# Attention by pairs of heads, with whole float32 score products on two halves of the array's rows

## The chip, the cores and the metric

The kernel runs on one core of a Trainium2 chip. The core has a matrix engine (TensorE; in the profile PE for the products and PEld for loading their stationary operand), a vector engine (DVE), a scalar engine (ACT), GpSimd (POOL), and SyncE (SP), whose queue issues all the DMAs here. Each engine works through its own instructions in program order, and semaphores tie the engines together. The metric is the time of the whole program on the device in microseconds (us).

## The reference

Capped softmax attention over 4 batches of 12 heads (448 positions, head size 64), then two feed-forward networks over the 1792 tokens:

```python
scores = (q @ k.T) / sqrt(64)                    # per batch and head: 448 x 448
scores = cap * tanh(scores / cap)                # cap = 30
attn = exp(scores - max(scores, axis=-1))
attn = attn / (sum(attn, axis=-1) + 1e-09)
x = concat_heads(attn @ v)                       # 1792 x 768
h = maximum(x @ w_in, 0);  x = (h * h) @ w_out   # 768 -> 2048 -> 768
g = x @ w_gate                                   # 768 -> 1536
out = (g * sigmoid(g) * (x @ w_val)) @ w_out2    # 1536 -> 768
```

The weights arrive as 64-bit floats; inputs q, k, v and the output are float32.

## The kernel before

**Feed-forward.** A batch (448 tokens) is the moving operand, 128 x 128 blocks of weights are the stationary one. To keep float32 accuracy on the `float32r` path, weights and activations are split into a high and a low part (`w_hi`, `w_lo`; `x_hi`, `x_lo`; `g_hi`, `g_lo`), and `unit_mm` (L595) sums three products, high·high, high·low and low·high. There are 4896 such matmuls of 448 columns, in three passes over the weights: pass 0 takes batches 0 and 1 together and decodes the 64-bit weights on DVE (L563 to L565: three integer instructions a unit) while storing the decoded copy to DRAM; pass 1 takes batch 2 and pass 2 batch 3 with the stored copy.

**Attention.** Scores are kept transposed: keys on the partitions (4 chunks of 112), queries along the free axis. Per head (`h`), in two steps `u` of two key chunks each: `scores` (L266, or L263 for the very first pair of heads), `tanh` on ACT from PSUM (L168), the maximum over the chunks on DVE (`tree`, L176 and L177), the maximum over the 112 partitions on POOL (`reduce`, L186: 448 elements wide), subtraction on DVE (`sub`, L190), `exp` on ACT (L194). Then the row sums and the product with v (`av`, L286: two heads side by side in two 64-column halves of the array), the reciprocal (`recip`), `norm`, and the split into `x`.

Scores also go through `float32r`: `hi` (ACT, L136) and `lo` (DVE, L140) split q and k, and `stack` (L157) moves the parts by DMA, so that the 128 rows of the array hold the high part of 64 dimensions of one head over its low part. Two matmuls with the high and the low part of q on both halves give one 112 x 448 block, four give a step `u`. The PSUM tile `s` (two banks) has one buffer.

Batches 0 and 1 (12 pairs of heads) come before the feed-forward, with nothing else to do ("early" below). There q and k are transposed on PE (`early_tr`), the result of POOL is copied by ACT into PSUM (`early_m`, L271: tile `mp`), so `sub` reads one operand from SBUF and one from PSUM, and the row sums are products of `ones` with each chunk (`row_sum`, L302). Batches 2 and 3 ("late") are spread between the feed-forward matmuls of passes 0 and 1; there q and k are transposed on DVE, `sub` reads the tile `mr` in SBUF, and DVE adds the four chunks up (`total`, L314 and L316) before one product with `ones` a head (`total_sum`, L324).

**What sets the order.** `early_attention` is a list schedule with a table of priorities (`PRIO`): an operation goes to its engine when its inputs and buffers are free by the table's durations. The late attention and the feed-forward are laid out by times: `plan_head` puts each step at an offset (`STEP`) from the time of its scores, and all events are emitted sorted by time.

Of the kernel before, what the change touches and what calls it, by code (L numbers as in the profile page):

```python
# [18 lines left out]
DRAM = bass.MemoryType.DRAM  # L19


@with_exitstack
def kernel(
# [17 lines left out]

    nc = tc.nc
# [11 lines left out]


    PRIO = dict(
        st=-1276.1, stj=95.8, ld=-54.4, lv=478.5, tr=-26.9, sc=-34.5, tree=-70.1, par=1194.4,
        m=-55.8, sub=50.5, exp=-11.6, av=-67.0, rc=253.2, norm=140.7, xh=261.1, w=-9.5,
        ws=462.4, wi=27.3,
    )  # L60
    STEP = dict(
        ld=-46.02, ldv=-8.42, pr=-14.3, st1=2.7, u1=2.2, mx=2.99, par=7.2, exp=2.5, av=5.6, av1=1.1,
        tot=1.86, sm=2.3, rs=6.8, rs1=6.18,
    )
    LEAD, TAIL = [17.2, 15.7], [60.0, 35.0]
    WEIGHT = [{'1b': 0.6, '2b': 0.6, 'end': 0.0}, {'end': 1.0}]
    NPRE, NWARM, GB = 3, 50, 10
    LAG = 0.2
# [33 lines left out]
    c_abs = capt[:CP, 1:2]  # L102
    c_inv = capt[:CP, 2:3]


    MM = S / 2.4e3 + 0.003
    EARLY = 2
    raw_t, pair_t, head_t = {}, {}, {}
    v_busy = [False, False]
    x_done = {}  # L110

    def att_load(b, p):
        kr = ap.tile([P, TB, 32], F32, tag="kr", name="kr")
        qr = ap.tile([P, TB, 32], F32, tag="qr", name="qr")
        for t, src in ((kr, k), (qr, q)):
            for j in range(2):
                for e in range(2):
                    g = 2 * j + e
                    nc.sync.dma_start(
                        t[32 * g : 32 * g + 32],  # L120
                        src[b, 2 * p + j, :, 32 * e : 32 * e + 32].rearrange("(t r) d -> r t d", r=32),
                    )
        raw_t[b, p] = dict(k=kr, q=qr)

    def att_tr(b, p, x):
        d = raw_t[b, p]
        d[x + "T"] = ap.tile([P, S], F32, tag="tT", name=x + "T")
        V.transpose(out=d[x + "T"], in_=d[x].rearrange("p t d -> p (t d)"))

    def src_t(b, p, x):  # L130
        d = raw_t[b, p]
        return d["ps" + x][:, :S] if b < EARLY else d[x + "T"]
# [11 lines left out]
    def stack(b, p, x, j):  # L144
        hl = f32(raw_t[b, p]["hl" + x])
        r = slice(64 * j, 64 * j + 64)
        if x == "k":
            t = ap.tile([P, S], F32R, tag="ks", bufs=4, name="ks")
            src = (hl[r, 0], hl[r, 1])
        elif b < EARLY:  # L150
            t = fp.tile([P, 2, S], F32R, tag=f"acc{j}", bufs=3, name="qs")
            src = (hl[r], hl[r])
        else:
            t = ap.tile([P, 2, S], F32R, tag="qs", bufs=2, name="qs")
            src = (hl[r], hl[r])
        for i in range(2):
            nc.sync.dma_start(f32(t[64 * i : 64 * i + 64]), src[i])  # L157
        head_t.setdefault((b, 2 * p + j), {})[x] = t

    def att_begin(b, h):  # L160
        t = ap.tile([CP, NC, S], F32, tag="al" if h % 2 else "ah", name="tt")
        head_t[b, h]["t"] = [t[:, 2 * i : 2 * i + 2] for i in range(2)]

    def tanh(b, h, u):
        d = head_t[b, h]
        if b < EARLY:
            d.setdefault("t", []).append(fp.tile([CP, 2, S], F32, tag="g", bufs=GB, name="te"))
# [28 lines left out]
    def x_hi(b, c, src):
        A.copy(xbuf[b % 2][c][:, 0], src())

    def x_lo(b, c, src, on=None):
        x = xbuf[b % 2][c]  # L200
        (on or V).tensor_tensor(x[:, 1], src(), f32(x[:, 0]), ALU.subtract)  # L201
        x_done[b, c] = x_done.get((b, c), 0) + 1


    def early_load(b, p):
        raw_t[b, p] = {}
        if (b, p) == (0, 0):
            n = ap.tile([CP, 2, 2, NC, D], F32, tag="ah", name="kqn")
            for j in range(2):
                for x, src in (("k", k), ("q", q)):  # L210
                    raw_t[0, 0][x] = n[:, "kq".index(x)]
                    nc.sync.dma_start(raw_t[0, 0][x][:, j], src[0, j].rearrange("(p c) d -> p c d", c=NC))
            return
        n = ap.tile([CP, 2, NC, 2, D], F32, tag="al" if p % 2 else "ah", name="kqn")
        for x, src in (("k", k), ("q", q)):
            t = raw_t[b, p][x] = n[:, "kq".index(x)]
            nc.sync.dma_start(t, src[b, 2 * p : 2 * p + 2].rearrange("j (p c) d -> p c j d", c=NC))

    def load_v(b, p):
        order = "j (p c) d -> p j c d" if b < EARLY else "j (c p) d -> p j c d"  # L220
        nc.sync.dma_start(vt[p % 2], v[b, 2 * p : 2 * p + 2].rearrange(order, c=NC))
        assert not v_busy[p % 2]
        v_busy[p % 2] = True
        pair_t[b, p] = dict(v=vt[p % 2])

    def transposes(pt, x, src):
        for c in range(NC):
            col = slice(c * CP, (c + 1) * CP) if x == "k" else slice(c, S, NC)
# [639 lines left out]
```

## Time and profile before

| | |
|---|---|
| three runs, median (lowest to highest) | 1274.63 us (1272.74 to 1274.97) |
| the profiled execution | 1278.07 us, its span 1276.3 us |
| PE busy | 1238.7 us, 97% of the span |
| DVE busy | 925.9 us, 73% |
| ACT busy | 586.9 us, 46% |
| POOL busy | 83.7 us, 7% |
| mean granted clock of TensorE | 0.988 |
| chain that ended last | PE 83%, DVE 9%, DMA 3%, ACT 3% |
| feed-forward matmuls in that chain (L595) | 70% |

A matmul's length in the profile includes the time until its result leaves the array, so neighbours overlap; what a matmul costs its successors is the distance between starts. A whole float32 matmul shows as two records, each of one part of the product; the order of instructions counts it once. Shares over the whole span mix the early stage, in which PE has gaps, with the later ones, in which it has nearly none, so the stages are to be read apart.

### The profile page before, as it was taken

How to read it: one execution, taken by the hardware profiler on the slowest of the kernel's cores; microseconds unless marked ns; L12 is line 12 of the kernel's file. 1: busy time of each engine (PE TensorE's matmuls, PEld its weight loads, DVE VectorE, ACT ScalarE, POOL GpSimd, SP SyncE). 2: the span in 40 equal slices, each digit the busy share in tenths (PEclk: the TensorE clock that was granted, in tenths of full speed). 3: DMA queues.
4: the chain of work that ended last, by engine and by line, in shares of the span. 5: the costliest groups of instructions: out<-in, count | busy, mean ns of one | idle time of the engine just before them, and what ended most of it. 6: DMA issues, size and time to landing. Idle time of an engine off the chain costs nothing.

```text
span 1276.3 us, 17347 instructions
## 1 busy us (share of the span) xinstructions
PE 1238.7 (97%) x6348; PEld 1048.2 (82%) x6348; DVE 925.9 (73%) x1449; ACT 586.9 (46%) x895; POOL 83.7 (7%) x59
## 2 busy tenths in 40 slices
PE   7889899999999899999999999999999999999997
PEld 5544469889798699898898988897898899999997
DVE  5899987767877887779888756887866833465344
ACT  4788765435334324333142376554454354433431
POOL 1223210000001001001000010010010000000000
PEclk8999899999999899999999999999999999999999
DMA  7877627556573575874765875457354443343333
GB/s 177 212 176 181 152 69 202 160 166 182 149 221 108 146 208 137 231 183 113 236 168 131 228 154 145 121 141 165 103 135 121 113 125 112 107 127 105 108 91 85
DMA packets 235365, 191.28 MB, mean 150 GB/s; under 512 B 144336, under 2 KB 197904, under 8 KB 235280
## 3 DMA queue, kind: packets, MB, share of 16 engines
q1 hardware_dynamic: 235280, 190.17, 55.6%
q8 instruction: 50, 0.82, 0.3%
q14 instruction: 35, 0.29, 0.1%
HBM read 124.85 MB, written 33.62 MB: 124 GB/s over the span
## 4 chain that ended last, share of the span: by engine, by line
PE 83%; DVE 9%; DMA 3%; ACT 3%; issue 2%; SPq 1%; DVEq 0%; POOL 0%; POOLq 0%; ACTq 0%
PE ff L595 70%; PE sc L266 5%; PE av L286 5%; DVE te L190 1%; PE rs L302 1%; DMA qs<-hl 1%; PE rs L324 1%; DVE mx L176 1%; DVE wp L582 1%; DVE acc L641 1%; DVE x L201 1%; ACT te L168 1%; DVE wx L564 1%; PE tr L229 1%; ACT te L194 1%
## 5 line engine op out<-in xcount | busy, mean ns | idle before, releaser
L595 PE MATMUL ff<-x,wp 128*128 128x448 f32 x2880 | 595.3, 365 | 1.4 <-DVE x L201 1.4
L595 PEld LDWEIGHTS ff<-x,wp 128*128 128x128 f32 x2880 | 538.9, 188 | 52.3 <-issue 6.4
L595 PE MATMUL ff<-g,wp 128*128 128x448 f32 x2016 | 420.5, 367 | 1.5 <-DVE g L633 1.5
L595 PEld LDWEIGHTS ff<-g,wp 128*128 128x128 f32 x2016 | 378.2, 188 | 42.1 <-issue 7.8
L582 DVE TENSOR_TENSOR wp<-wx,wp 128x768 fp32r<-128x768 f32 (+1 forms) x246 | 207.7, 844 | 139.7 <-ACT wp L577 134.7
L577 ACT CAST wp<-wx 128x768 fp32r<-128x768 f32 (+1 forms) x246 | 177.5, 722 | 253.3 <-PE ff L595 161.4
L186 POOL PARTITION_ALL_REDUCE mr<-mx x48 | 81.2, 1692 | 902.4 <-DVE mx L177 869.3
L266 PE MATMUL sc<-qs,ks 128*112 128x448 f32 x368 | 95.2, 381 | 15.6 <-ACT te L168 11.6
L641 DVE TENSOR_TENSOR acc<-ff,acc 128x448 f32<-128x448 f32 x120 | 74.0, 618 | 41.0 <-PE ff L595 40.6
L266 PEld LDWEIGHTS sc<-qs,ks 128*112 128x112 f32 x368 | 61.9, 178 | 42.5 <-ACT te L168 21.6
L633 DVE TENSOR_TENSOR g<-gg,g 128x448 fp32r<-128x448 f32 x112 | 69.3, 618 | 13.7 <-ACT g L629 13.5
L629 ACT CAST g<-gg 128x448 fp32r<-128x448 f32 x112 | 63.1, 564 | 34.4 <-DVE gg L625 33.8
L610 ACT ACTIVATE r<-ff 128x448 f32<-128x448 f32 x64 | 34.8, 544 | 84.4 <-PE ff L595 84.2
L616 ACT ACTIVATE th<-ff 128x448 f32<-128x448 f32 x48 | 26.1, 544 | 96.7 <-PE ff L595 96.6
L564 DVE SCALAR_TENSOR_TENSOR wx<-wr,wx 128x512 int32<-128x512 int32 (+1 forms) x82 | 68.1, 830 | 2.8
L565 DVE SCALAR_TENSOR_TENSOR wx<-wr,wx 128x512 int32<-128x512 int32 (+1 forms) x82 | 67.4, 822 | 2.8
L620 DVE SCALAR_TENSOR_TENSOR sg<-th,ff 128x448 f32<-128x448 f32 x48 | 29.7, 619 | 52.8 <-ACT th L616 52.8
L168 ACT ACTIVATE te<-sc,capt 112x896 f32<-112x896 f32 x48 | 48.2, 1004 | 28.7 <-PE sc L266 21.3
L625 DVE SCALAR_TENSOR_TENSOR gg<-ff,sg 128x448 f32<-128x448 f32 x48 | 29.9, 622 | 36.7 <-PE ff L595 36.4
L194 ACT ACTIVATE tt<-tt,capt 112x896 f32<-112x896 f32 x48 | 48.9, 1042 | 7.4 <-DVE tt L190 7.4
L639 ACT COPY acc<-ff 128x448 f32<-128x448 f32 x48 | 25.6, 534 | 56.1 <-PE ff L595 56.1
L194 ACT ACTIVATE te<-te,capt 112x896 f32<-112x896 f32 x48 | 48.9, 1038 | 5.2 <-DVE te L190 4.9
(63 smaller groups left out, 818.3 us busy)
## 6 DMA issues: line engine op xcount, KB each, us to landing
wx<-w SPq DMA_DIRECT2D x80, 384.0 KB, 3.1
wx<-w SPq DMA_DIRECT2D x84, 256.0 KB, 2.6
qs<-hl SPq DMA_DIRECT2D x92, 224.0 KB, 3.8
w<-wx SPq DMA_DIRECT2D x40, 384.0 KB, 2.7
wr<-in_moe_w_in_dram SPq DMA_DIRECT2D x16, 768.0 KB, 5.5
wr<-in_moe_w_out_dram SPq DMA_DIRECT2D x24, 512.0 KB, 4.1
w<-wx SPq DMA_DIRECT2D x42, 256.0 KB, 2.2
ks<-hl SPq DMA_DIRECT2D x92, 112.0 KB, 2.9
```

Of the source, the lines that this page charges most:

```text
L186: G.partition_all_reduce(d["m"], d["mx"][:, 0], CP, bass_isa.ReduceOp.max)
L194: A.activation(t, t, AF.Exp, scale=c_abs)
L266: PE.matmul(ps[:CP, i, :S], d["k"][:, cols], d["q"][:, s], start=(s == 0), stop=(s == 1))
L286: PE.matmul(d["ps"][64 * j : 64 * j + 64, :S], d["v"][:, j, c], head_t[b, 2 * p + j]["t"][u][:, c % 2], start=(c == 0), stop=(c == NC - 1),)
L564: V.scalar_tensor_tensor(x, hi, -0x40000000, x, ALU.bitwise_and, ALU.bitwise_or)
L565: V.scalar_tensor_tensor(x, lo, 29, x, ALU.logical_shift_right, ALU.bitwise_or)
L577: A.copy(hl[:, 0], raws[ps, i])
L582: (on or V).tensor_tensor(hl[:, 1], raws[ps, i], f32(hl[:, 0]), ALU.subtract)
L595: PE.matmul(ffn_ps[i, b][:, :S], hl[:, h, c], x[:, t], start=(c == 0 and s == 0), stop=(c == cnt(u) - 1 and s == 2),)
L629: A.copy(g_t[b, f][:, 0], tmp_t[i, b])
L633: (on or V).tensor_tensor(g[:, 1], tmp_t.pop((i, b)), f32(g[:, 0]), ALU.subtract)
L641: V.tensor_tensor(acc, pt, acc, ALU.add)
```

## The change

- One class `Plan` replaces both ways of ordering: every operation of the program has an engine, a duration, a rank (its wished time), inputs and buffers, and `order` hands out the earliest operation that can start.
- Attention works on a pair of heads at a time. q and k of a pair lie in one tile `kT` (128 partitions: head 0 on the lower 64, head 1 on the upper), copied from PSUM by ACT in the early stage, transposed by DVE in the late one. `hi`, `lo`, `stack` and their DMAs are gone.
- `scores` (L228) does one key chunk of both heads: two whole float32 matmuls with 64 contraction rows each, in the lower and the upper row half of the array, each into a PSUM bank of its own. In the early stage, chunks take turns between the PSUM tiles `s` and `a`.
- Maximum, reduction, subtraction, exponential and (late) sum work on 112 x 896 tiles, both heads side by side: three `top` (L245), one `reduce` (L250) of 896 elements, four `sub` (L256) a pair; late, three `total` (L282) and one group of four sum matmuls (L290) just ahead of the eight `av` matmuls (L303).
- `sub` reads the reduced maximum from SBUF in both stages; the copy to PSUM is gone.
- The decode of a unit's weights is three operations instead of one, pass 0 starts with three units of batch 0 and then three of batch 1, and passes 1 and 2 load weights into five buffers instead of four.

```diff
+class Plan:
+    def order(self, free):
...
+        while len(seq) < len(ops):
+            best = None
+            for eng, some in ready.items():
+                first = None
+                for i in some:
+                    _, _, _, rank, _, _, _, alloc, _ = ops[i]
+                    t = max(since[i], free[eng])
...
+                    if t < 1e9 and (first is None or (t, rank) < first[:2]):
+                        first = t, rank, i
+                if first and (best is None or (first[0], first[2]) < (best[0], best[2])):
+                    best = first
...
-    def hi(b, p, x):
-        t = raw_t[b, p]["hl" + x] = ap.tile([P, 2, S], F32R, tag="hl", bufs=2, name="hl")
-        A.copy(t[:, 0], src_t(b, p, x))
-
-    def lo(b, p, x):
-        t = raw_t[b, p]["hl" + x]
-        V.tensor_tensor(t[:, 1], src_t(b, p, x), f32(t[:, 0]), ALU.subtract)
...
+    def tr_copy(b, p, i):
+        A.copy(kt(b, p)[:, i], pair[b, p].pop(("tr", i))[:, :S])
...
+    def scores(b, p, c, tag):
+        d = pair[b, p]
+        pool = ps_s if tag == "s" else ps_a
+        ps = d["s", c] = pool.tile([P, 2, 512], F32, tag=tag, name="sc")
+        for j in range(2):
+            r = slice(64 * j, 64 * j + 64)
+            PE.matmul(
+                ps[:CP, j, :S], d["kT"][r, 0, c * CP : (c + 1) * CP], d["kT"][r, 1], start=True, stop=True
+            )
...
-    def tree(b, h):
...
-        V.tensor_tensor(mx, d["t"][0], d["t"][1], ALU.max)
-        V.tensor_tensor(mx[:, 0], mx[:, 0], mx[:, 1], ALU.max)
...
+    def top(b, p, c):
+        d = pair[b, p]
+        if c == 1:
+            d["mx"] = ap.tile([CP, 2, S], F32, tag="mx", bufs=2, name="mx")
+        V.tensor_tensor(d["mx"], d["t", 0] if c == 1 else d["mx"], d["t", c], ALU.max)
...
+    def sub(b, p, c):
+        d = pair[b, p]
+        V.tensor_tensor(d["t", c], d["t", c], d["m"], ALU.subtract)
...
-    def early_m(b, h):
-        d = head_t[b, h]
-        ps = ps_a.tile([P, 512], F32, tag=f"a{h % 2}", name="mp")
-        A.copy(ps[:CP, :S], d["m"])
-        d["m"] = ps[:CP, :S]
...
+    def total(b, p, c):
+        d = pair[b, p]
+        if c == 1:
+            d["sm"] = ap.tile([CP, 2, S], F32, tag="mx", bufs=2, name="sm")
+        V.tensor_tensor(d["sm"], d["t", 0] if c == 1 else d["sm"], d["t", c], ALU.add)
...
+    def total_sum(b, p):
+        d = pair[b, p]
+        d["a"] = ps_a.tile([P, 2, 512], F32, tag="a", name="av")
+        d["rs"] = d["a"][:, 1]
...
+            add(K("sc", c), "PE", 0.78, at + 8 + c, scores, (b, p, c, tag), deps, [(tag, 1, [K("th", c)])], pe)
...
+        add(K("par"), "POOL", 3.2, at + 13, reduce, (b, p), [K("top", 3)], [("m", 2, [K("sub", 3)])])
```

Where the work stands is shown at two places. The first is PE in pass 0, at the first late pair of heads (`ff` are feed-forward products, `sc` scores, `rs` row sums, `sm` the sums that DVE made, `av` the product with v). Before:

```order
L266 MATMUL sc<-qs,ks 112x448 x4
L595 MATMUL ff<-g,wp 128x448 x12
L266 MATMUL sc<-qs,ks 112x448 x4
L595 MATMUL ff<-g,wp 128x448 x36
L266 MATMUL sc<-qs,ks 112x448 x4
L595 MATMUL ff<-g,wp 128x448 x12
L266 MATMUL sc<-qs,ks 112x448 x4
L595 MATMUL ff<-g,wp 128x448 x48
L324 MATMUL rs<-sm,ones 32x224 x2
```

and now, from the third scores group of the pair on:

```order
L228 MATMUL sc<-kT 112x448 x2
L453 MATMUL ff<-x_0_85,wp 128x448 x3
L453 MATMUL ff<-x_1_86,wp 128x448 x3
L453 MATMUL ff<-x_2_87,wp 128x448 x3
L228 MATMUL sc<-kT 112x448 x2
L453 MATMUL ff<-x_3_88,wp 128x448 x3
L453 MATMUL ff<-x_4_89,wp 128x448 x3
L453 MATMUL ff<-x_5_90,wp 128x448 x3
L453 MATMUL ff<-g,wp 128x448 x63
L290 MATMUL av<-sm,ones 32x224 x4
L303 MATMUL av<-tt,v 64x448 x8
```

The four scores groups of a pair stood 12 to 36 feed-forward matmuls apart and now stand 9 apart; the sums, two groups before (the second between the two halves of `av`), are one group ahead of `av`, 72 feed-forward matmuls behind the last scores.

The second place is DVE in the early stage, about pairs 2 to 4 (`mx` maximum, `te` and `tt` tanh tiles, `mp` and `mr` the reduced maximum in PSUM and in SBUF, `hl` the low part of q or k, `st`, `rc`, `rb` the reciprocal, `xs` and `x_n` the output of attention). Before:

```order
L176 TENSOR_TENSOR mx<-te 112x896
L177 TENSOR_TENSOR mx<-mx 112x448
L140 TENSOR_TENSOR hl<-tr,hl 128x448 x2
L201 TENSOR_TENSOR x_2_83<-xs,x_2_83 128x448
L190 TENSOR_TENSOR te<-te,mp 112x896 x2
```

and now:

```order
L245 TENSOR_TENSOR mx<-mx,tt 112x896
L245 TENSOR_TENSOR mx<-te 112x896
L315 STREAM_TRANSPOSE st<-rs 128x224
L319 TENSOR_SCALAR rc<-st 128x14
L322 TENSOR_SCALAR rc<-st 32x7 x4
L326 RECIPROCAL rc<-rc 128x14
L329 STREAM_TRANSPOSE rb<-rc 128x448
L245 TENSOR_TENSOR mx<-mx,te 112x896
L256 TENSOR_TENSOR te<-te,mr 112x896 x2
```

The last maximum of a pair (the first row of each piece ends or holds it) releases POOL's reduction; what DVE did meanwhile mostly read a PSUM operand (`tr`, `mp`), and is now another pair's maximum, with both operands in SBUF.

## Rows read from the trace of the kernel before

**Rows 1.** Stages: window, length, then busy us (instructions) by engine, PEclk, DMA share, GB/s.
```profile
20.00:180.00 160.00, 142.66 (x969) 82.10 (x967) 147.36 (x246) 122.01 (x160) 38.75 (x24) 0.96 0.67 159
416.00:428.00 12.00, 8.53 (x30) 3.65 (x29) 10.50 (x17) 4.33 (x7) 0.00 (x0) 0.72 0.44 136
428.00:722.00 294.00, 294.00 (x1457) 262.20 (x1456) 239.83 (x376) 95.04 (x145) 10.08 (x6) 1.00 0.65 178
```

**Rows 2.** Waits of PE after 200 us: who for whom, total us, times, longest.
```profile
PE rs L324 <- DVE sm L316: 4.1, 2, 3.5
```

**Rows 3.** Groups of DVE: line, operation, tiles, shapes, count | busy us, mean ns.
```profile
L140 DVE TENSOR_TENSOR hl<-tr,hl 128x448 fp32r<-128x448 f32 x22 | 13.0, 615 | 2.8 <-ACT hl L136 2.8
L176 DVE TENSOR_TENSOR mx<-te 112x896 f32<-112x896 f32 x24 | 26.1, 1086 | 5.4 <-ACT te L168 5.2
L177 DVE TENSOR_TENSOR mx<-mx 112x448 f32<-112x448 f32 x48 | 30.0, 625 | 1.7
L190 DVE TENSOR_TENSOR te<-te,mp 112x896 f32<-112x896 f32 x48 | 49.6, 1078 | 0.4 <-ACT mp L271 0.4
L190 DVE TENSOR_TENSOR tt<-tt,mr 112x896 f32<-112x896 f32 x48 | 50.7, 1085 | 0.0
```

**Rows 4.** PE in order of time at 308 us: start us, length us, instruction.
```profile
307.32 0.77 PE L595 MATMUL ff<-x,wp 128*128 128x448 f32 x3
307.93 0.97 PE L266 MATMUL sc<-qs,ks 128*112 128x448 f32 x4
308.74 0.57 PE L595 MATMUL ff<-x,wp 128*128 128x448 f32 x2
```

**Rows 5.** The same view at 335 us.
```profile
334.87 1.72 PE L286 MATMUL av<-tt,v 112*64 112x448 f32 x8
336.53 0.57 PE L324 MATMUL rs<-sm,ones 112*32 112x224 f32 x4
337.03 1.72 PE L286 MATMUL av<-tt,v 112*64 112x448 f32 x8
338.69 0.47 PE L595 MATMUL ff<-g,wp 128*128 128x448 f32 x1
```

**Rows 6.** Within the first row of that group, from three narrow windows.
```profile
334.87 0.60 PE L286 MATMUL av<-tt,v 112*64 112x448 f32 x2
...
335.30 0.92 PE L286 MATMUL av<-tt,v 112*64 112x448 f32 x4
...
335.68 0.92 PE L286 MATMUL av<-tt,v 112*64 112x448 f32 x4
```

**Rows 7.** PE near the start: whole float32 scores of the first pair.
```profile
15.98 1.76 PE L263 MATMUL sc<-qs,ks 96*112 96x448 f32 x4
17.58 1.05 PE L482 MATMUL warm<-zero 128*128 128x128 f32 x8
```

**Rows 8.** DVE and POOL in order of time, in four windows.
```profile
61.23 1.08 DVE L190 TENSOR_TENSOR te<-te,mp 112x896 f32<-112x896 f32 x1
61.48 1.60 POOL L186 PARTITION_ALL_REDUCE mr<-mx  x1 [5.18 <-DVE mx L177]
...
307.22 3.04 POOL L186 PARTITION_ALL_REDUCE mr<-mx  x1 [83.25 <-DVE mx L177]
...
319.03 1.83 POOL L186 PARTITION_ALL_REDUCE mr<-mx  x1 [8.77 <-DVE mx L177]
319.50 1.17 DVE L316 TENSOR_TENSOR sm<-sm,tt 112x448 f32<-112x448 f32 x1
...
320.70 0.62 DVE L316 TENSOR_TENSOR sm<-sm,tt 112x448 f32<-112x448 f32 x1
```

**Rows 9.** PE around the longest of its late waits.
```profile
421.55 0.96 PE L324 MATMUL rs<-sm,ones 112*32 112x224 f32 x4 [3.47 <-DVE sm L316]
422.45 3.25 PE L286 MATMUL av<-tt,v 112*64 112x448 f32 x8
425.63 2.54 PE L595 MATMUL ff<-g,wp 128*128 128x448 f32 x7
```

More of the change, by code (lines that the diff above doesn't have):

```diff
@@ L1 @@
-import heapq
 import math
@@ L53 @@
     FG = 4
[L56 to L68, printed above, removed]
+    EARLY = 2
+    GB, TBUF, NPRE, NWARM = 10, 4, 3, 30
+    FIRST = [17.0, 16.0]
+    LAST = [60.0, 35.0]
     const = ctx.enter_context(tc.tile_pool(name="const", bufs=1))
@@ L100, in set_cap @@
         V.tensor_scalar(capt[:, 2:3], capt[:, 2:3], QS, None, ALU.mult)
[L102 to L118, printed above, removed]
+    pair = {}
@@ L196, in x_hi @@
[L196 to L228, printed above, removed]
-            PE.matmul(pt[:, col], src(c), ident[:CP, :CP], start=True, stop=True, is_transpose=True)
@@ L328, in total_sum @@
+    def total_sum(b, p):
+        d = pair[b, p]
+        d["a"] = ps_a.tile([P, 2, 512], F32, tag="a", name="av")
+        d["rs"] = d["a"][:, 1]
+        for g in range(4):
+            j, i = divmod(g, 2)
+            PE.matmul(
+                d["rs"][32 * g : 32 * g + 32, : S // 2],
+                ones,
+                d["sm"][:, j, i * (S // 2) : (i + 1) * (S // 2)],
                 start=True,
@@ L479, in warm @@
[L479 to L494 removed]
+        d = pair.pop((b, p))
@@ L759, with warm @@
-    early, end = early_attention()
-    t_ffn = max(end[k] for k in end if k[0] in ("av", "mm"))
-    rel = {x: [-1e9] * 3 for x in ("wp", "wr", "wx")}
-    rel["wrx"], rel["wrp"] = [], []
-    t = 0.0
-    for t0, o in early:
-        at(t0 - t_ffn, o["fn"], *o["a"])
-        if o["eng"] == "PE" and t0 > t_ffn:
-            on_pe(t0 - t_ffn, lambda now, d=o["dur"]: d)
+    warm_t = {}
+    def warm(i):
+        if i == 0:
+            warm_t[0] = ps_f.tile([P, 512], F32, tag="f", name="warm")
+        PE.matmul(warm_t[0][:, :P], zero, zero, start=True, stop=True)
@@ L768 @@
+    PAIR = 7.6
+    steps = []
+    t = T0 = 11.0 * EARLY * KD + 8.0
+    gates = {}
     for ps, (bs, seq) in enumerate(passes):
[L769 to L770 removed]
         order = [(i, b) for i in range(NB) for b in bs]
         if ps == 0:
[L773 to L784 removed]
+            order = [(i, b) for b in bs for i in range(NPRE)] + order[NPRE * len(bs) :]
+        lens = [MM3 * cnt(seq[i]) for i, _ in order]
+        heads, spent, at = 0, 0.0, t
+        room = sum(lens) - FIRST[min(ps, 1)] - LAST[min(ps, 1)]
@@ new lines @@
+    for ps, i, b, _ in steps:
+        users.setdefault((ps, i), []).append(b)
+    add(("ident",), "POOL", 8.0, -99, lambda: None)
+    add(("cap",), "DVE", 0.8, -99, set_cap, (), [])
+    for n in range(EARLY * KD):
+        plan_pair(n, 10.6 * n)
+    for i in range(NWARM):
+        add(("warm", i), "PE", 0.43 if i < 8 else 0.22, 1e4 + i, warm, (i,), [("warm", i - 1)] if i else [],
+            [("f", 4, [("warm", NWARM - 1)])] if i == 0 else [])
+    for n, (step, at) in sorted(gates.items()):
+        plan_pair(n, at - 10.0, [("mm", *step[:3], 0)])
@@ L841 @@
+    with tc.manual_schedule():
+        V.memset(zero, 0.0)
+        make_identity(nc, ident)
+        nc.sync.dma_start(capt[:, 0:1], cap[None, :].to_broadcast([P, 1]))
+        G.memset(ones, 1.0)
+        seq = plan.order(dict(PE=0.4, ACT=2.0, DVE=2.6, POOL=0.5, SP=0.0))
+        for _, n in seq:
+            plan.ops[n][4](*plan.ops[n][5])
 _INS = ["q", "k", "v", "cap", "moe_w_in", "moe_w_out", "moe2_w_gate", "moe2_w_val", "moe2_w_out"]
```

854 lines of the change are left out of this document (379 added, 475 removed).

## The prediction

> **What bounds the kernel now.** I read the busy time by stage first, since shares over the span mix unlike stages. From 428 to 722 us PE is busy in all of its 294 us; there only work taken off PE counts. From 20 to 180 us DVE is the fuller engine, 147.36 of 160 us, and PE stands at 142.66 with its overlapping tails counted in [rows 1]. So the early attention goes at DVE's pace, and what DVE does for a pair of heads sets the time, while late only PE's own work and its waits do. Second I read who waits for whom after 200 us: PE waits 4.1 us in all for the sums that DVE makes, 3.5 us of them at once [rows 2]. [...] The `av` group then takes 3.25 us instead of 1.72, the row sum 0.96 instead of 0.57 [rows 5, 9]. Third come the groups of DVE by shape, and last the order in time at PE, for what a visit of attention costs between feed-forward matmuls.
>
> **Early: what DVE loses and gains.** Per pair before: two low parts at 13.0/22 = 0.59 us, two wide maxima at 26.1/24 = 1.09, two narrow ones at 30.0/48 = 0.63, four subtractions at 49.6/48 = 1.03, in sum 8.73 us [rows 3]. Now: three wide maxima, 3.26, and four subtractions from an operand in SBUF, 50.7/48 = 1.06 each [rows 3], 4.22: 7.48 us. The rest (reciprocal, norm, split of x) is the same. 12 pairs x 1.25 us = 15.0 us less.
>
> Against that stands POOL. At 61.48 us a reduction runs 1.60 us beside a subtraction that reads PSUM, and the subtraction takes its usual 1.08 us. At 319.03 us another runs beside a sum of two SBUF operands: that takes 1.17 us, and the same instruction behind it 0.62 [rows 8]. So a reduction of 448 elements holds such an instruction for 0.55 us. Before, the early stage hardly met this: its subtractions read the PSUM copy, its low parts the PSUM transposes. Now the subtractions read SBUF, and the reduction is 896 wide. In the order of DVE, in 9 of 12 early pairs the instruction behind the last maximum reads two SBUF operands. The trace has no 896-wide reduction. The bounds are 0 (as at 61.48) and two holds of twice the length, 2.2 us a pair; I take one hold of twice the length in 9 of 12 pairs, 0.83 us, nearest to the row at 319.50: 12 x 0.83 = 9.9 us. Early net: -15.0 + 9.9 = -5.1 us.
>
> [...]
>
> The transposes' copies go from ACT and DVE to ACT alone, the PSUM copies of the maximum leave ACT; ACT is busy 122.01 of 160 us [rows 1], so I count nothing. If DVE's pace fell to ACT's, the 15.0 could not be had in full. DVE also idles 12.6 us from 20 to 180 us [rows 1]. Without the DMAs of `stack` behind q and k, and with two PSUM tiles for the scores, some of that goes, but three engines are now close to each other in load, and the order of each is fixed beforehand: -2 us, between 0 and -6.
>
> **Late: PE's visits.** Matmuls of 448 columns follow each other at 0.203 us (307.32 to 307.93, three). A scores visit of four costs 308.74 - 307.93 = 0.81 us [rows 4]. In the whole float32 `av`, two products start together in the two column halves, and the next two 0.38 us later (335.30 to 335.68) [rows 6]; a float32 product is two such parts. No row shows two row halves at once; the nearest is this pair of column halves. From it, the two products of a scores visit take 2 x 0.38 = 0.76 us. Entering and leaving such a layout costs something too: from the end of the slot before 334.87 to 338.69 there are 8 steps of `av` and two half steps of sums, 9 x 0.38 = 3.42 of 3.82 us [rows 5], so 0.4 us for the changes, and I take 0.14 each. A visit is then 0.76 + 0.28 = 1.04 us: 48 late visits x 0.23 = +11.0 us. The upper bound is the halves one behind the other: at the start two whole float32 score products take 17.58 - 15.98 = 1.60 us [rows 7]; with the changes 1.88.
>
> The sums and `av` of a pair were one visit of about 3.9 us [rows 5] and one lone sum visit of about 0.6 (one step of 0.38 and two changes). Now one visit: one step, 8 steps of `av`, three changes, 9 x 0.38 + 0.42 = 3.8. That is -0.7 x 12 = -8.4 us. Late visits: +2.6 us.
>
> **Late: the wait for the sums.** Behind the last scores PE has 72 feed-forward matmuls, 14.6 us, and the visit's 1.04: 15.7 us. The chain that has to fit: scores 1.2 with their tail, tanh taken as long as a subtraction, 1.1, last maximum 1.09, reduction 2 x 1.60 [rows 8], four subtractions 4.2, three sums of 896 at the price of a maximum, 3.3: 14.1 us, and DVE's weight work comes in between, as do POOL's holds. If a sum is late, all of PE's feed-forward stands behind it in order. I take 0.5 us a pair, 6 us (bounds 0 and 18). What goes is the one long wait and its slow stretch: 4.1 [rows 2] plus 1.5 for `av`, 0.4 for the sums and 1.0 for seven feed-forward matmuls that take 2.54 us [rows 9], 7.0 us. Net -1.0.
>
> **Sum.** -5.1 - 2 + 2.6 - 1.0 = -5.5 us. The profiled execution has 1278.07 us (span 1276.3), which is 3.4 above the median of the runs; it becomes 1272.6, and the median 1274.63 becomes 1269.
>
> **Rivals.**
> *The row halves take turns.* For it: no row shows them together. Against: the column halves do run together [rows 6], and the two products write different PSUM banks. Price: 48 x (1.88 - 0.81) = +51, sums -8.4, and early 0.84 us x 4 more of PE a pair, 40 us against 17 us of gaps [rows 1], so DVE's gain turns to some +10: near 1325 us. It decides from a visit of about 1.1 us on.
>
> *POOL and DVE hold each other (the slower side).* Place: the early chain maximum, reduction, subtraction, and the same chain late. For it: at 307.22 us a reduction took 3.04 us instead of 1.60 [rows 8], so POOL is held as well. Price: two holds of 1.1 us a pair early, 26.4 - 15.0 = +11.4; late a reduction of up to 2 x 3.04 lengthens the chain by 2.9 us, of which I let 1.5 reach PE, 18 - 7.0 = +11; visits +2.6, idle -2: +23, 1298 us. It decides from 1.25 us lost a pair. Against it: most reductions stay at 1.60 us. [...]
>
> *More is gained.* One hold of 0.55 in 9 of 12 pairs (5 us, early -10), half of DVE's idle time gone (-6), no late wait (-7.0), visits +2.6: -20, 1254 us. For it: DVE's late load falls too, since its low parts go there as well.
>
> **How the numbers follow.** Forecast 46%, with 1258 to 1277 as its own range; turns of the row halves 12%; the hold of POOL and DVE 27%; more gained 15%. Below 0.2%, 2.5 us, a measurement of this kernel can't tell a difference from none. Faster: three quarters of the forecast and all of the last, 0.50; within: 0.10, out of the forecast's middle and the mildest holds; slower: 0.40. The range 1250 to 1305 leaves out the turns of the row halves and the ends of the others.
>
> **What would show it.** Scores records in pairs that start within some ns of each other, and visits near 1.04 us; if they start 0.38 us or more apart, the first rival. Subtractions and maxima of 1.1 us, and about 2 us where POOL runs; POOL's reductions near 3.2 us. Twelve late visits of sums and `av` near 3.8 us, with waits for `sm` of some tenths. DVE busy some 5 us less in the early stage, the last early `av` some 5 us earlier. I am wrong if the early stage moves by more than 10 us either way, or if PE waits late for over 1 us a pair.

## The result, and the profile after

The changed kernel takes 1293.93 us (median of 4 runs, 1290.72 to 1296.38) against 1274.80 for the kernel before beside it: ratio 1.0147, interval [1.0116, 1.0177]. Forecast was 1269: it became slower, not faster. The profiled execution has 1293.31 us, span 1291.3, so 15.2 us more than before.

I compared the two traces at the same feed-forward matmul. At the 91st, where the early attention is over, the changed kernel is 4.2 us ahead (183.72 us against 187.94). At the 3672nd, the end of pass 1, it is 15.5 us behind (1035.62 against 1020.11), and at the end 14.6. So the early stage gained, and the late one lost 19.7 us.

The stages after (window, length, busy us and instructions by engine, PEclk, DMA share, GB/s), to be read against [rows 1]:

```profile
20.00:180.00 160.00, 137.08 (x887) 52.40 (x886) 153.67 (x219) 106.79 (x133) 41.34 (x12) 0.93 0.26 65
428.00:722.00 294.00, 291.64 (x1421) 249.98 (x1421) 227.43 (x341) 91.40 (x138) 8.60 (x3) 1.00 0.55 157
```

Early, DVE is busy 6.3 us more of the 160, though it has less to do. Late, DVE has less to do, and PE is still the engine that sets the time. The same 294 us hold 36 matmul records fewer.

**Who waits for whom late.** Waits of PE after 200 us (total us, times, longest):

```profile
PE av L303 <- DVE st L315: 7.8, 12, 1.1
PE av L290 <- DVE sm L282: 3.8, 2, 2.6
```

The second row is the wait of [rows 2], nearly unchanged (4.1 before). The first was not there before: in every late pair, `av` stands still in the middle of its visit. PE and DVE in order of time around one of the twelve:

```profile
314.73 0.59 PE L290 MATMUL av<-sm,ones 112*32 112x224 f32 x8
315.25 0.97 PE L303 MATMUL av<-tt,v 112*64 112x448 f32 x4
316.83 2.48 PE L303 MATMUL av<-tt,v 112*64 112x448 f32 x12 [0.61 <-DVE st L315]
319.24 1.49 PE L453 MATMUL ff<-x,wp 128*128 128x448 f32 x6
...
315.60 0.62 DVE L492 TENSOR_TENSOR g<-gg,g 128x448 fp32r<-128x448 f32 x1
316.27 0.42 DVE L315 STREAM_TRANSPOSE st<-av 128x224 f32<-128x224 f32 x1
316.72 0.17 DVE L319 TENSOR_SCALAR rc<-st 128x14 f32<-128x14 f32 x1
```

Both the sums (second bank) and the product with v (first bank) live in one PSUM tile, `a`. In the order of the program `st`, which reads the sums, comes behind the first chunk of `av` (in the first late pair behind the second). Here DVE is busy with `g` until 316.22, so this piece alone does not tell why `st` starts at 316.27. In nine of the other eleven visits DVE stands idle ahead of `st`. At 404 us it does so for 1.00 us, though the sums were through at 402.96, and what ends its wait is `av`:

```profile
404.70 0.42 DVE L315 STREAM_TRANSPOSE st<-av 128x224 f32<-128x224 f32 x1 [1.00 <-PE av L303]
```

So `st` waits for a chunk of `av` that it does not read, and the next chunk waits until `st` has read (316.69), as it would if dependencies were kept for the tile as a whole; runs 1 and 2 test that. Before, sums and `av` were two tiles [rows 5].

I measure a visit as in the prediction: from the start of the last feed-forward matmul ahead to the next one behind, less one slot of 0.2035 us. Visits of sums and `av` have a median of 4.60 us now, against 3.90 + 0.59 before in two visits.

**The scores.** One visit in order of time, against [rows 4], and a narrow window on its first two records:

```profile
287.18 1.81 PE L453 MATMUL ff<-g,wp 128*128 128x448 f32 x8
288.92 1.01 PE L228 MATMUL sc<-kT 64*112 64x448 f32 x4
289.86 1.48 PE L453 MATMUL ff<-g,wp 128*128 128x448 f32 x6
...
288.92 0.63 PE L228 MATMUL sc<-kT 64*112 64x448 f32 x2
```

The second row of scores comes from the window 288.88 to 288.95: both heads' products have begun, so the row halves work side by side. In all 48 late visits the two start 0.01 us apart. The median visit has 1.03 us (before 0.81). Behind it the second gap between feed-forward matmuls is 0.31 us instead of 0.20; behind the scores on the whole array before it was 0.20.

**Early DVE.** Groups of DVE from 20 to 180 us (count, busy us, mean ns), first after, then before:

```profile
L256 DVE TENSOR_TENSOR te<-te,mr 112x896 f32<-112x896 f32 x36 | 39.0, 1117 | 0.0
L322 DVE TENSOR_SCALAR rc<-st 32x7 f32<-32x7 f32 x48 | 15.6, 326 | 0.9
L319 DVE TENSOR_SCALAR rc<-st 128x14 f32<-128x14 f32 x12 | 9.8, 819 | 0.4
```

```profile
L343 DVE TENSOR_SCALAR rc<-st 32x7 f32<-32x7 f32 x48 | 9.4, 196 | 0.9
L340 DVE TENSOR_SCALAR rc<-st 128x14 f32<-128x14 f32 x12 | 2.6, 220 | 0.2
```

The same small instructions of the reciprocal take 25.4 us instead of 12.0. The trace says where (DVE, then POOL):

```profile
132.96 0.41 DVE L315 STREAM_TRANSPOSE st<-rs 128x224 f32<-128x224 f32 x1
133.41 1.51 DVE L319 TENSOR_SCALAR rc<-st 128x14 f32<-128x14 f32 x1
134.95 1.67 DVE L322 TENSOR_SCALAR rc<-st 32x7 f32<-32x7 f32 x4
136.66 0.24 DVE L326 RECIPROCAL rc<-rc 128x14 f32<-128x14 f32 x1
...
133.21 2.86 POOL L250 PARTITION_ALL_REDUCE mr<-mx  x1 [16.93 <-DVE mx L245]
```

Beside one reduction the five instructions take 3.18 us; away from any, at 125.67 us, 0.17 + 0.69. Such an instruction reads one operand in SBUF, not two. I call an instruction's length beyond the median of its kind its hold. Summed over all DVE instructions that lie beside a reduction, the early hold is 21.2 us, 15.6 of them in these small instructions, against 3.7 before.

The forecast put the hold on the instruction behind the last maximum. In nine of the twelve early pairs that one does read two SBUF operands, but it starts 0.2 to 0.3 us ahead of the reduction and keeps its usual length. Of those that start while a reduction runs, four take 1.3 to 1.5 us more and the others nothing. Once both kinds stand side by side (DVE, then POOL):

```profile
107.93 1.08 DVE L245 TENSOR_TENSOR mx<-te 112x896 f32<-112x896 f32 x1
109.11 2.38 DVE L245 TENSOR_TENSOR mx<-mx,te 112x896 f32<-112x896 f32 x1
...
108.18 3.56 POOL L250 PARTITION_ALL_REDUCE mr<-mx  x1 [9.97 <-DVE mx L245]
```

**Two pitches.** In long stretches without attention, feed-forward matmuls follow each other at 0.2027 or at 0.2067 us, and in the changed kernel they stay at one until the next visit. (In the kernel before, the pitch also changes several times within pass 2, where there are no visits: between 0.2022 and 0.2067 us, taken over 60 matmuls each.) From 220 to 289 us and from 410 to 478 us, among others, the changed kernel goes at the longer: 1116 of 4644 such matmuls (before 558 of 4422), counted in blocks of six. Between the 91st and the 3672nd matmul it is 1092 now and 132 before.

### The profile page after: what moved, and what is told of

It is laid out like the page before. It is cut to its first block, busy times and chain, and to the rows that moved or that the text cites. A ratio compares the mean times of both kernels' runs of the same rounds, so it can differ in the third digit from the quotient of the medians.

```text
span 1291.3 us, 16640 instructions
## 1 busy us (share of the span) xinstructions
PE 1246.6 (97%) x6300; PEld 996.8 (77%) x6300; DVE 906.4 (70%) x1341; ACT 568.6 (44%) x847; POOL 78.7 (6%) x31
## 4 chain that ended last, share of the span: by engine, by line
PE 83%; DVE 13%; issue 1%; ACT 1%; SPq 0%; DMA 0%; DVEq 0%; ACTq 0%
PE ff L453 73%; PE av L303 4%; PE sc L228 4%; DVE mx L245 3%; DVE te L256 2%; DVE tt L256 1%; DVE rc L322 1%; DVE rc L319 1%; DVE sm L282 1%; PE warm L521 1%; DVE st L315 1%; PE rs L269 1%; DVE rb L329 1%; DVE wp L442 1%; DVE x L348 0%
## 5 line engine op out<-in xcount | busy, mean ns | idle before, releaser
L437 ACT CAST wp<-wx 128x512 fp32r<-128x512 f32 (+1 forms) x246 | 176.9, 723 | 204.2 <-PE ff L453 141.4
L442 DVE TENSOR_TENSOR wp<-wx,wp 128x512 fp32r<-128x512 f32 (+1 forms) x246 | 206.8, 843 | 52.5 <-ACT wp L437 47.7
L250 POOL PARTITION_ALL_REDUCE mr<-mx x24 | 77.9, 3247 | 926.3 <-DVE mx L245 926.3
L228 PE MATMUL sc<-kT 64*112 64x448 f32 x384 | 93.7, 580 | 12.7 <-ACT te L239 10.9
L239 ACT ACTIVATE tt<-sc,capt 112x896 f32<-112x896 f32 x60 | 60.5, 1008 | 57.5 <-PE sc L228 57.3
L228 PEld LDWEIGHTS sc<-kT 64*112 64x112 f32 x384 | 27.9, 173 | 49.8 <-issue 22.7
L260 ACT ACTIVATE tt<-tt,capt 112x896 f32<-112x896 f32 x60 | 60.0, 1038 | 10.3 <-DVE tt L256 10.3
L303 PE MATMUL av<-tt,v 112*64 112x448 f32 x240 | 55.6, 576 | 7.8 <-DVE st L315 7.8
L256 DVE TENSOR_TENSOR tt<-tt,mr 112x896 f32<-112x896 f32 x60 | 62.1, 1084 | 1.1 <-POOL mr L250 1.1
L484 DVE SCALAR_TENSOR_TENSOR gg<-ff,sg 128x448 f32<-128x448 f32 x48 | 29.9, 623 | 33.8 <-PE ff L453 33.7
```

The costliest lines, as they stand in the source:

```text
L228: PE.matmul(ps[:CP, j, :S], d["kT"][r, 0, c * CP : (c + 1) * CP], d["kT"][r, 1], start=True, stop=True)
L250: G.partition_all_reduce(d["m"].rearrange("p j s -> p (j s)"), d["mx"].rearrange("p j s -> p (j s)"), CP, bass_isa.ReduceOp.max)
L256: V.tensor_tensor(d["t", c], d["t", c], d["m"], ALU.subtract)
L303: PE.matmul(d["av"][64 * j : 64 * j + 64, :S], d["v"][:, j, c], d["t", c][:, j], start=(c == 0), stop=(c == NC - 1),)
L437: A.copy(hl[:, 0], raws[ps, i])
L442: V.tensor_tensor(hl[:, 1], raws[ps, i], f32(hl[:, 0]), ALU.subtract)
```

## The experiments

All are edits of the changed kernel; times are medians beside runs of the kernel before (1273.2 to 1274.7 us).

| kernel | us (lowest to highest, runs) | ratio to before |
|---|---|---|
| two_tiles | 1279.58 (1276.68 to 1286.66, 9) | 1.0041 [1.0023, 1.0059] |
| av_first | 1273.47 (1272.64 to 1275.08, 12) | 0.9995 [0.9983, 1.0006] |
| two_chunks | 1280.71 (1277.01 to 1281.64, 7) | 1.0044 [1.0028, 1.0060] |
| late_f32r | 1292.78 (1289.90 to 1294.72, 5) | 1.0146 [1.0125, 1.0168] |
| after_again | 1293.46 (one run) | |
| av_first_two_chunks | 1269.60 (1267.62 to 1271.28, 8) | 0.9962 [0.9948, 0.9976] |
| av_first_f32r | 1276.54 (1272.76 to 1279.41, 12) | 1.0013 [1.0001, 1.0025] |
| twice_reduced | 1327.71 (1326.37 to 1331.00, 4) | 1.0423 [1.0403, 1.0443] |
| recip_direct | 1278.36 (1275.42 to 1281.39, 12) | 1.0023 [1.0009, 1.0037] |
| two_chunks_later | 1272.76 (1270.36 to 1275.50, 12) | 0.9984 [0.9971, 0.9997] |
| all_together | 1261.81 (1261.71 to 1261.90, 4) | 0.9891 [0.9874, 0.9907] |
| av_chunks_recip | 1257.18 (1257.03 to 1257.35, 4) | 0.9875 [0.9863, 0.9888] |
| whole_array_after | 1261.45 (1260.12 to 1265.27, 6) | 0.9917 [0.9902, 0.9933] |

**1. The sums in a tile of their own.**

```diff
-        d["rs"] = d["a"][:, 1]
+        d["rs"] = ps_s.tile([P, 2, 512], F32, tag="s", name="rs")[:, 0]
```

> Only the late row sums move, from the second bank of the PSUM tile a to a tile of the pool s. Theory (av stands behind the sums because DVE's transpose st reads the tile that av writes): the twelve waits of av for st (7.8 us in the changed kernel) go, a visit of sums and av falls from a median of 4.60 us to about 3.9 us, and the time falls by 7 to 9 us, to about 1285 us. Rival (POOL and DVE hold each other, and the wait for st only shows that DVE comes late): DVE is as late as before, the wait moves to sm or to the next scores, and the time stays within 2 us of 1294 us.

It falls by 14.4 us, more than expected. The waits for `st` are gone, those for `sm` are not (waits of PE after 200 us):

```profile
PE rs L290 <- DVE sm L282: 3.9, 2, 2.6
PE sc L228 <- DVE kT L220: 0.2, 1, 0.2
```

The median visit is 3.77 us, and the twelve together take 49.4 us instead of 62.7: 13.3 of the 14.4. Of these, 12 x 0.83 = 10.0 are the waits for `st`. Another 3.0 come from the visit with the longest wait for `sm`: PE waits as long as in the changed kernel (2.62 us there), but here the granted clock stays at 1.00 behind the wait, and the visit takes 6.45 us instead of 10.24:

```profile
401.33 0.58 PE L290 MATMUL rs<-sm,ones 112*32 112x224 f32 x8 [2.61 <-DVE sm L282]
401.84 3.23 PE L303 MATMUL av<-tt,v 112*64 112x448 f32 x16
```

The rival said within 2 us; it is out.

**2. The same tile, but `av` ahead of the sums.**

```diff
-deps = [ex c, lv, av c-1, rs]           # av
+deps = [ex c, lv, av c-1 or tot 3]      # av; total_sum now depends on av 3
```

> The tile stays one, but the late av come ahead of the sums in the same visit. Theory: av waits for neither st nor sm, since the sums are the last thing in the visit; the visit has a median of about 3.9 us, the 3.8 us of waits for sm shrink to under 1.5 us because 3.3 us of av now cover them, and the time falls by 8 to 11 us, to about 1284 us. Rival (DVE late through POOL): the sums at the end wait as much as they did at the start, and the time falls by less than 3 us.

It falls by 20.5 us, to the time of the kernel before. Among the waits of PE after 200 us neither `st` nor `sm` is left; the first row is now:

```profile
PE sc L228 <- DVE kT L220: 0.3, 1, 0.3
```

A visit in order of time, and behind it feed-forward at once:

```profile
312.29 3.23 PE L305 MATMUL av<-tt,v 112*64 112x448 f32 x16
315.45 0.58 PE L289 MATMUL av<-sm,ones 112*32 112x224 f32 x8
315.97 2.30 PE L455 MATMUL ff<-x,wp 128*128 128x448 f32 x10
```

All twelve visits have 3.76 to 3.77 us, 45.2 in sum: 17.5 less. 12 x 0.83 = 10.0 of it are the waits for `st`. Of the other 7.5, 6.9 are in the two visits in which the changed kernel waited for `sm` too, and 0.6 in one where `st` came later still. The pitch gave 2.9 more in this trace (378 matmuls at the longer one against 1116). The longest wait for `sm` had PE idle for 2.62 us, and the granted clock was 0.50 in the 6.70 us behind it (in the changed kernel: PE in order of time, then the window behind):

```profile
402.08 0.88 PE L290 MATMUL av<-sm,ones 112*32 112x224 f32 x8 [2.62 <-DVE sm L282]
405.26 4.34 PE L303 MATMUL av<-tt,v 112*64 112x448 f32 x12 [0.61 <-DVE st L315]
```

```profile
402.30:409.00 6.70, 6.09 (x22) 1.70 (x16) 5.13 (x14) 0.00 (x0) 0.00 (x0) 0.50 0.09 30
```

That the visit has one length wherever DVE stands, once nothing in it depends on `st`, is what tells the tile from a late DVE.

**3. Two key chunks in a visit of late scores.**

```diff
-            tag = "a" if early and c % 2 else "s"
+            tag = "a" if c % 2 else "s"      # and sc 2 waits for th 1
```

> Late scores take turns between the tiles s and a, as the early ones do, so that a visit has two key chunks: 24 late visits of scores instead of 48, the same products. Theory (a visit costs 0.28 us of changes of layout plus 0.1 us in the second gap behind it): a visit of two chunks has about 1.8 us instead of 2 x 1.03, and 24 second gaps of 0.1 us go: 24 x (0.28 + 0.1) = 9 us less, about 1285 us. Rival (the cost of scores is all in the products, none in the changes): a visit has 2.06 us and the time stays within 2 us of 1294 us.

It falls by 13.2 us. A visit of two chunks has 1.78 us as expected (1.76 long in the row below), 2 x 1.03 - 1.78 = 0.28 less, 6.8 in sum. All scores visits take 45.4 us instead of 51.7, and visits of sums 58.3 instead of 62.7, by waits that fell elsewhere. Only 30 matmuls went at the longer pitch, which gives 4.3 more in this trace. Run 5 shows that such stretches move from one run to the next, so I take that for luck.

```profile
291.98 1.76 PE L228 MATMUL sc<-kT 64*112 64x448 f32 x8
293.67 2.69 PE L453 MATMUL ff<-g,wp 128*128 128x448 f32 x12
```

**4. The late scores by split parts again.**

```diff
+ hi (ACT), lo (DVE), stack (8 DMAs a pair) of kT; then, for both heads of a chunk:
-  PE.matmul(ps[:CP, j, :S], kT[r, 0, chunk], kT[r, 1])
+  for s in range(2): PE.matmul(ps[:CP, j, :S], ks[j][:, chunk], qs[j][:, s], start=(s == 0), stop=(s == 1))
```

> The late scores alone go back to the split of q and k into high and low parts, stacked by DMAs, four matmuls on the whole array for a key chunk of both heads; all else stays. Theory: 48 visits fall from 1.03 to 0.81 us (-10.7 us), their second gaps of 0.1 us go (-4.8 us), and the feed-forward behind them runs at its shorter pitch (0.2027 us instead of 0.2067 in a fourth of the matmuls, up to -4 us); the waits for st stay: about 1277 us, between 1272 and 1281. Rival (POOL and DVE hold each other): DVE gets four more instructions of 0.6 us a late pair and is later still, the waits for sm and st grow, and the time falls by less than 8 us.

The visits are 0.81 us as expected, but the time stays: six of them wait for the stacking DMAs or run slowly behind such a wait (10.0 of the 11.5 us that the visits take over the median), and the sums come later (visits of sums 67.5 us, waits for `sm` 6.4). The total sides with the rival's number; most of the waits are my plan's, which gave a pair of DMAs 0.8 us on SP where they take 1.4 to 1.8 (at 570 us). Run 7 repairs that.

**5. The changed kernel again.**

> The changed kernel once more, unchanged, to see what of its trace is chance. Theory: the waits of av for st (about 7.8 us) and the sizes of the visits (1.03 and 4.60 us) are the same, while the stretches in which the feed-forward matmuls follow each other at 0.2067 us instead of 0.2027 lie elsewhere, so that the time moves by up to 3 us either way. Rival (the pitch belongs to places of the program): the same stretches are slow again, those from 220, 410, 508 and 783 us.

Visits are alike (1.03, 4.60), the slow stretches elsewhere: this time pass 2. The same 220 us in this window, first of the earlier trace, then of this one:

```profile
1030.00:1250.00 220.00, 220.00 (x1087) 203.93 (x1086) 106.50 (x153) 94.88 (x158) 0.00 (x0) 1.00 0.38 113
```

```profile
1030.00:1250.00 220.00, 220.00 (x1067) 199.79 (x1066) 102.17 (x147) 93.49 (x157) 0.00 (x0) 1.00 0.37 109
```

220 / 1087 = 0.2024 us a matmul, 220 / 1067 = 0.2062, at the same granted clock of 1.00. So the pitch is not tied to places of the program. That puts anything from 0.1 us (30 such matmuls, run 3) to 7 us (1764, run 10) into a single trace.

**6. Runs 2 and 3 together.**

> The late av ahead of the sums, and two key chunks in a late visit of scores. Theory: both gains are PE's time and add: from the 1273.5 us of av first, 24 visits of 1.78 instead of 48 of 1.03 us (-6.8) and 24 fewer second gaps of 0.1 us (-2.4): about 1264 us, between 1260 and 1268. Rival (the two changes took away the same waits of PE): the second adds less than 3 us, 1271 us or more.

It gains 3.9 us on top of av_first, not the expected 9: the scores visits take 45.6 us instead of 52.0, but 1398 matmuls went at the longer pitch (378 in the trace of av_first), 4.0 us. In spite of that it is faster than the kernel before.

**7. Split scores with `av` first.** The edit is that of run 4 on run 2, with 1.7 us planned on SP for each pair of DMAs.

> The late scores by split parts on the whole array again, now with av ahead of the sums and with 1.7 us planned on SP for each pair of stacking DMAs (the earlier such kernel planned 0.8, and its scores stood waiting for them). Theory (a whole float32 scores visit costs 1.03 + 0.1 us, one by parts 0.81): from the 1273.5 us of av first, 48 x 0.32 = 15 us less if PE now waits for nothing, about 1259 us; with 5 us of waits left, 1264. Rival (DVE's four more instructions a pair come back as PE's waits for the sums): over 1270 us.

46 visits have a median of 0.81 us, yet the time is 3.1 us above av_first: PE waits 5.0 us for DVE's `x`, and two visits of `av` take 7.4 and 4.5 us instead of 3.77. The trace, 2.9 us above the median of its runs, also has 1608 matmuls at the longer pitch against 378, which is 4.9 us. So the cheaper visits are real, and the rival's number came. That DVE's added work eats the gain, as the rival has it, is shown in part only.

**8. POOL's work doubled.**

```diff
+        for j in range(2):
+            G.partition_all_reduce(twice, d["mx"][:, j], CP, bass_isa.ReduceOp.max)
```

> The changed kernel with the work of POOL doubled: behind each reduction of 896 elements two of 448 whose results nobody reads, so POOL runs twice as long beside DVE, and nothing waits for it but POOL's next reduction and the tile mx. Theory (a reduction holds DVE for 0.7 us, which early is on the path and late mostly not): 12 x 0.7 = 8 us early and 0 to 6 us late through later sums, so 1301 to 1308 us. Rival (the hold of POOL and DVE is what made the change slower than forecast): as much again as the change lost against its forecast, 20 us or more, over 1313 us.

33.8 us more; my price was far too low, and by number the rival wins. 21.7 of it are early; late, the visits of sums and `av` take 74.3 us instead of 62.7. The groups of rows above, from 20 to 201 us:

```profile
L325 DVE TENSOR_SCALAR rc<-st 32x7 f32<-32x7 f32 x48 | 30.2, 630 | 0.9
L322 DVE TENSOR_SCALAR rc<-st 128x14 f32<-128x14 f32 x12 | 10.4, 870 | 0.4
```

The reciprocal's instructions grew once more, to 40.6 us, and the early hold to 38.0. This drew my eye to them and led to run 9.

**9. The reciprocal without TENSOR_SCALAR.**

```diff
-            V.tensor_scalar(d["rc"], s..., 1e-9, None, ALU.add)
+            V.reciprocal(d["rc"], s...)
-                V.tensor_scalar(d["rc"][...], s[32 * g : 32 * g + 32], 1e-9, None, ALU.add)
+                V.reciprocal(d["rc"][...], s[32 * g : 32 * g + 32])
```

> The changed kernel with the five small tensor_scalar instructions of a pair's reciprocal (they add 1e-9 and swap the halves) made into five RECIPROCAL instructions, which leaves the 1e-9 and the sixth instruction out. Theory (in the changed kernel POOL's reduction holds DVE mostly in these small instructions, 1.51 us instead of 0.17 and 1.67 instead of 0.69 at 133 us, about 15 us over the early pairs; a RECIPROCAL beside the reduction, that of 0.24 us at 136.66, starts after its end, so that whether it is held is not known): if RECIPROCAL is not held, DVE has 12 to 18 us less early and PE's early stage ends 8 to 14 us sooner, 1280 to 1286 us. Rival (any small DVE instruction is held alike): within 4 us of 1294 us, less only by the 12 x 0.24 us of the instruction left out.

It falls by 15.6 us. In the trace 10.6 us are gained by the 91st feed-forward matmul (173.16 against 183.72 us). The same place of the program (DVE, then POOL), with the reduction beside:

```profile
126.87 0.41 DVE L315 STREAM_TRANSPOSE st<-rs 128x224 f32<-128x224 f32 x1
127.32 0.24 DVE L319 RECIPROCAL rc<-st 128x14 f32<-128x14 f32 x1
127.59 0.81 DVE L322 RECIPROCAL rc<-st 32x7 f32<-32x7 f32 x4
...
127.12 2.86 POOL L250 PARTITION_ALL_REDUCE mr<-mx  x1 [16.74 <-DVE mx L245]
```

RECIPROCAL is not held (0.241 to 0.244 us for all 24 of the wider form in the span), and the early hold is 5.4 us. The rival is out: the same small operands are held under TENSOR_SCALAR and not under RECIPROCAL.

**10. The first late pair later** (run 6 with `FIRST = [24.0, 16.0]` and longer planned loads).

> The kernel with av ahead of the sums and two key chunks a visit, with the first late pair planned 39 feed-forward matmuls later. Theory (the first late scores stand 3.6 us for the transposes of q and k, whose DMAs come in the rush at the end of the early stage, and PE goes at its lower clock for a few us behind them): these 3 to 5 us go, from 1269.6 to about 1265.5 us. Rival (the DMAs are as late wherever the pair stands, since they are queued behind weights): the wait stays, within 1.5 us of 1269.6.

A miss: 3.2 us slower. The wait and its slow stretch are gone (scores visits 42.8 us instead of 45.6, every one near 1.78). But the whole order moved with it: at 842 to 857 us PE now waits 0.9 us for `sm` and 1.9 for `x`, and 1764 matmuls went at the longer pitch.

**11. With run 9's reciprocals.**

> The last kernel with the reciprocals of recip_direct as well. Theory: what recip_direct gains adds to it, since early and late are apart: about 1255 us, between 1250 and 1260. Rival (small instructions are held alike): within 3 us of the last kernel.

10.95 us below run 10, 1.1% below the kernel before. At the 91st feed-forward matmul it is 10.0 us ahead (173.55 against 183.59), so the early gain adds to the late one.

**12. The version that the runs point to:** runs 2, 3 and 9, the first late pair at its old place.

> The sum of what has gained: av ahead of the sums, two key chunks a late visit, the reciprocals by RECIPROCAL alone (the 1e-9 left out), and the first late pair where the changed kernel has it. Theory (the early 15.6 us of recip_direct and the late gains are apart): 1269.6 - 15.6 = about 1254 us, between 1250 and 1258. Rival (the first late pair's place matters, and the later place in all_together was part of its gain): 1262 us or more.

1257.18 us, 12.4 below run 6 and 1.25% below the kernel before. It leaves out the 1e-9.

```profile
20.00:180.00 160.00, 143.24 (x934) 59.90 (x931) 145.49 (x220) 112.66 (x146) 40.93 (x12) 0.96 0.31 75
428.00:722.00 294.00, 293.99 (x1445) 255.10 (x1444) 226.77 (x335) 95.50 (x147) 9.64 (x3) 1.00 0.59 162
```

Early, DVE has 8 us less in the window than in the changed kernel, and PE does 47 records more.

**13. A small whole-array product behind each late visit.**

```diff
+        PE.matmul(t[:, 0, 448:512], zero, zero[:, :64], start=True, stop=True)
```

> The same kernel with one small product on the whole array (zeros, 128 rows, 64 columns, into unused PSUM columns) as the last thing in each of the 36 late visits. Theory (after a visit that ends in a part of the array, feed-forward goes on at one of two pitches by chance, 0.2027 or 0.2067 us; after one that ends on the whole array, as the scores of the kernel before, at the shorter): no stretch behind these visits runs at 0.2067, the second gap of 0.1 us goes, and the small product itself costs 0.1 to 0.2 us: between -4 and +3 us against the kernel without it, with less spread. Rival (the pitch has nothing to do with what ends a visit): as many slow matmuls as in the other kernels, 400 to 1800, and 4 to 7 us slower for the added products.

4.3 us slower. Visits grew by 0.25 us, 36 x 0.25 = 9, and the pitch gave 3.8 back: 738 matmuls at the longer pitch against 1704. The second gap behind a visit stayed at 0.29 us. Slow stretches still begin behind these visits, one of 318 matmuls at 573 us. The rival's number came. My theory that the end of a visit decides is not borne out; what does stays open.

## Why the prediction was wrong, point by point

Forecast -5.5 us, measured +15.2 in the profiled executions: 20.7 apart. In its own terms (measured sums are mine, from the order of starts in the two traces):

| term | forecast | measured |
|---|---|---|
| early, DVE's work, hold and idle time | -7.1 | -4.2 |
| scores visits | +11.0 | +11.8 |
| visits of sums and `av`, regular part | -8.4 | +1.2 |
| late waits for sums and their slow stretches (measured: within the visits) | -1.0 | +1.4 |
| feed-forward between visits | 0 | +5.3 |
| pass 2 and the ends | 0 | -0.3 |

- **The step that failed** is "Now one visit: one step, 8 steps of `av`, three changes, 9 x 0.38 + 0.42 = 3.8. That is -0.7 x 12 = -8.4 us." The size of PE's work was right: 3.77 us, in runs 1 and 2. It left out that the two share a PSUM tile, so that a DVE instruction stands between two chunks of `av`: 0.83 us x 12 = 10.0 us. This miss alone turns the forecast's sign (-5.5 + 9.6). With the wait removed the change is still 0.4% slower than before (run 1), and level with it where the waits for `sm` go too (run 2).
- **The scores** came as computed: side by side, 1.03 us against 1.04. Only the sum agrees: the two parts of a product start 0.47 us apart, not 0.38. What I missed is the second gap behind a visit on part of the array, 0.1 us. The rival that the halves take turns is out.
- **Early**, -15.0 for DVE's list fits the lengths away from a reduction (1.08 and 1.09 us), but a second step failed: "I take one hold of twice the length in 9 of 12 pairs". The hold was +9.9 forecast, 21.2 - 3.7 = 17.5 measured, 1.46 us a pair, and none of it lies where I put it. Those nine instructions start ahead of the reduction and keep their length; most of the hold fell on TENSOR_SCALAR, with one SBUF operand. Such a hold did not last as long as the reduction: at 133.41 us an instruction begun 0.20 us into a reduction of 2.86 us was through after 1.51. Why these instructions are held and others are not, no run shows. That DVE stood idle 6.3 us of the 160 and not 12.6 (I took 2 us off) hid much of it. The rival that POOL and DVE hold each other decided from 1.25 us a pair on, so its condition was met; its price was not: the early stage still gained 4.2 us, and the reductions kept 3.25 us (78 us for 24), not up to 6. That its 1298 us lies near the measured time is luck. So this hold is a real loss, shown by runs 8 and 9, but the early term missed by 2.9 us and the visit's by 9.6.
- **Late waits for sums**: 3.8 us in two waits, as before, not a spread of tenths over twelve pairs. In the changed kernel a slow stretch came behind the longer of them too: a granted clock of 0.50 from 402.30 to 409.00 us, behind a wait of 2.62 us. Run 1 has a wait of 2.61 us at the same place and a granted clock of 1.00 behind it, so such a stretch cannot be counted on.
- **Feed-forward between visits**: +3.8 us from the longer pitch (1092 matmuls against 132), +3.6 from 36 more second gaps of 0.1 us, -2.8 for waits of before that went, and 0.7 spread over the rest. No term stood for it. The pitch's part is chance as far as run 5 shows it, where this whole term is +1.7 us and pass 2 is 4.7 us longer instead. What the other parts of the change do (the order of the units, the decode in three operations, five weight buffers) no run takes apart. The first late pair adds 3.2 us, 2.2 of it counted with the scores: these wait 1.67 us for `kT`, and nine feed-forward matmuls behind them take 3.4 us, at a granted clock of 0.50:

```profile
189.27 1.01 PE L228 MATMUL sc<-kT 64*112 64x448 f32 x4 [1.67 <-DVE kT L220]
190.21 3.41 PE L453 MATMUL ff<-x,wp 128*128 128x448 f32 x9
```

```profile
190.70:193.90 3.20, 3.20 (x10) 2.40 (x11) 3.08 (x6) 1.60 (x3) 0.00 (x0) 0.50 0.59 172
```

## What to carry to other kernels

When two results move into one tile, list who reads the first while the second is still being written: here that reader was a wait in the middle of the writer's work in every late pair, 0.83 us in the mean, and the other order gave 20 us, with the other waits and the slow stretch that went with it. When a neighbour engine's work grows, ask of each instruction kind beside it whether it is held, the smallest too, and try another instruction that does the same. Sum visits by their distances between starts, and compare two kernels at the same instruction of the main stream, before believing a wait list.

## What the runs showed of the hardware that was not expected

- The two pitches of the feed-forward matmuls, 0.2027 and 0.2067 us at a granted clock of 1.00, in most kernels here each kept from one visit to the next, and different from run to run; cause open.
- The reciprocal's float32 TENSOR_SCALAR on SBUF is held by a reduction on POOL (for 128x14 1.51 us at 133.41, 0.17 away from any at 125.67; 0.82 in the mean of the early ones), RECIPROCAL of the same operands is not (0.241 to 0.244 us, run 9). The int32 TENSOR_SCALAR of the weight decode kept its length beside two early reductions (0.55 us at 29.88, 0.57 at 94.05), so the name of the instruction does not decide alone; what else does is open.
- In nine early pairs a DVE instruction with two SBUF operands starts 0.2 to 0.3 us ahead of the reduction. It keeps its length (1.08 us at 107.93), and the reduction takes longer: 3.09 to 4.96 us in those nine pairs, 2.86 in the other three.
- The second feed-forward matmul behind a visit on part of the array starts 0.1 us late (0.31 us behind the first instead of 0.20). A small product on the whole array at the visit's end left it 0.08 us late (run 13); cause open.
- Behind PE's longest wait for `sm`, at one place of the program, the granted clock was 0.50 in the changed kernel (2.62 us of waiting) and 1.00 in run 1 (2.61 us).
